# Loads of 128 rows, one load for keys, values and gates, stacked float32r scores from step 12, and a new order, in an mLSTM + MLP kernel

## The chip, the cores and the metric

The kernel runs on one core of a Trainium2 chip. The time is device microseconds of one launch of that core, and three timed runs and one profiled execution of the kernel before are at hand.

## The reference, cut to what matters

First a gated recurrent attention (mLSTM) over 768 tokens for 4 batches of 8 heads with 40 dimensions, then an MLP on its output with 320 inputs and 2048 hidden units.

```
for t in range(S):                       # C, n, m: state per batch and head
    m_new  = max(f[t] + m, i[t])
    C = exp(f[t] + m - m_new) * C + exp(i[t] - m_new) * v[t] k[t]^T
    n = exp(f[t] + m - m_new) * n + exp(i[t] - m_new) * k[t]
    y[t] = sigmoid(o[t]) * (C q[t]) / max(|n . q[t]|, 1)
h = x @ w_in                             # x: y with the heads side by side
out = (h * erf(softplus(h))) @ w_out
```

## The kernel before, in words

The recurrence is done in chunks of 128 tokens. A step `s` (0 to 23) is one chunk of one batch: `attention(s)`. Its scores, part `S` at L682, are eight products of 40 rows (keys against queries, one per head) in float32, each of which the chip runs as two instructions; the heads of a pair lie on rows 0 to 39 and 64 to 103. The scores are weighted on VectorE (L697), and `ph` multiplies them with the values (L719), adds the state's share (L715) and makes the state's update (L724). The result is gated (L759, L765), transposed on TensorE (`tr`, L777) and split into two float32r tiles `xh` and `xl` for the MLP.

The MLP takes two steps at a time (a block of 256 tokens) in two halves of the hidden units: 24 phases `f`. Each runs `up` (L990, eight float32r products of 256 columns for every 128 hidden units), a copy out of PSUM (`hb`, L999 on ScalarE or L1001 on VectorE), softplus and erf (L1009, L1013), their product with `h` (L1021), a split in two (`gh` L1027, `gl` L1032) and `dn` (L1067, L1068, L1070, of 320 columns). The first three phases (`FULL`) run `dn` in plain float32 instead (L1063). The weights arrive as 64-bit floats and are decoded piece by piece over the first 130 us: `val` on ScalarE (L810), `dec` and `hi`, `lo` on the engines that the sets `HI_DVE`, `LO_DVE` and `LO_PE` name; a `lo` in `LO_PE` is two products on TensorE (L833, L834).

A step's inputs come by three transfers, all issued on SP's queue: `load` (q and k, 104 rows of 4 KB, L566) and `loadv` (keys and values at L573, gates at L574). From step 4 on two more bring the decays (`dq`, L586), from step 8 on one more the cumulated gates (`bq`, L619). The store of the output is at L1094.

The order of the whole program is written by a planner, `Plan.issue`: each part has an engine, a cost and a due time (`target`, from `FIRST`, `PHASE` and `BEHIND`), `NUDGE` and `CLASS` shift due times of single parts, and a list simulation puts the parts in one fixed order per engine. Every engine, SP's queue among them, then works that order off without exchange. From step 9 on (`CLUSTER`) `tr` of step s-2, `S` of step s and `ph` of step s-1 are merged into one part `X` on TensorE. `CHAIN` fixes ScalarE's order of exponentials, softplus and erf.

The stacked form of the scores is in the code before, but for steps from `STACK = 24` on, so for none. It splits q and k into float32r parts, `hi` on ScalarE (`qkh`, L650) and `lo` on VectorE (`qkl`, L655), and ten transfers within SBUF (`stk`, L664 to L668) put hi, hi, lo of q over hi, lo, hi of k on 120 rows of one tile, so that one float32r product per head (L680) takes the place of L682.

Of the kernel before, what the change touches and what calls it, by code (L numbers as in the profile page):

```python
# [17 lines left out]
B, H, S, D = 4, 8, 768, 40  # L18
# [32 lines left out]
class Plan:  # L51
# [3 lines left out]
    RATE = 250.0  # L55
# [75 lines left out]
    def issue(self):  # L131
# [28 lines left out]
        for p in parts:  # L160
            p.late += NUDGE.get(p.name, CLASS.get(p.name.rstrip('0123456789'), 0.0) if int(p.name.lstrip('abcdefghijklmnopqrstuvwxyzSX_') or 0) >= CLUSTER else 0.0)
            for b in p.held:
                b.left += 1
# [105 lines left out]
FIRST = 43.4  # L269
PHASE = 17.5  # L270
BEHIND = 1.57
KEEP = {'raw': 2, 'qk': 2, 'kvo': 2}
HB_ACT = {0, 2, 3, 5}
HI_DVE = {'i00', 'i01', 'i31', 'o2', 'o4'}
BURST = {0, 2, 3, 6, 7, 8, 9, 10, 11, 12, 13, 14, 15, 16, 17, 18, 19, 20, 21, 22}
LO_DVE = {'i10', 'i21', 'o6', 'o9', 't2'}
LO_PE = {'i01', 'i20', 'o0', 't1', 't2', 't3'}
# [19 lines left out]
]  # L297
GL_POOL = {2, 4}
CLUSTER = 9
STACK = 24  # L300
CLASS = {}
PARTIAL = None
AFTER = 10
PREFER = 75.7
VG_POOL = {6, 7}
SK_ACT = {0, 1, 2}
Y_DVE = {0, 1, 5, 7}
NUDGE = {
# [57 lines left out]
def tile_mlstm_moe(  # L366
# [108 lines left out]
    def gate_chunk(c):  # L475
# [6 lines left out]
        @make(f'gload{c}', 'SP', 0.6, kb=128.0, new=[gtb], order=[step[4 * c - 6].S] if c > 1 else [])  # L482
        def load():
            v.gt = new(sb, [128, 2, L], F32, "gt")
            nc.sync.dma_start(v.gt, gates[:, :, c * L:(c + 1) * L])
# [716 lines left out]
```

## Time and profile before

| what | value |
|---|---|
| three runs | 481.88, 486.70, 486.58 us, median 486.58 |
| the profiled execution | 482.13 us, of which the span from first to last instruction is 480.4 us |
| mean granted TensorE clock | 0.985 of full speed |
| busy share of the span | TensorE 97%, weight loads 90%, VectorE 67%, ScalarE 69%, GpSimd 23% |
| moved by DMA | 51.01 MB, 106 GB/s over the span |

Busy times of TensorE are of pipelined instructions and overlap, so starts are compared, not durations. The profile's rows name an engine (PE is TensorE, PEld its weight loads, DVE VectorE, ACT ScalarE, POOL GpSimd, SP SyncE, which issues the transfers), a line of the kernel, an operation, and the tiles (output and inputs); x is a count. In brackets stands the idle time of the engine just before, and what ended it.

### The profile page before, as it was taken

What the parts mean: (1) busy time and instruction counts of PE and PEld (TensorE: products, weight loads), DVE (VectorE), ACT (ScalarE), POOL (GpSimd) and SP (SyncE); (2) the same over time, 40 slices, a digit from 0 to 9 for tenths busy, and PEclk for the clock granted to TensorE, in tenths of its full rate; (3) what the DMA queues carried; (4) which work ended last, traced back from release to release, by engine and by line L of the source; (5) the groups of instructions that cost most, each with busy time, mean ns of one, the idle gap of its engine ahead of it and who ended that gap; (6) DMA issues with size and microseconds to landing.
All of it is one profiled execution on the core that took longest, in us unless ns stands there. A gap on an engine that the chain in (4) does not pass through costs nothing.

```text
span 480.4 us, 13816 instructions
## 1 busy us (share of the span) xinstructions
PE 466.9 (97%) x6081; PEld 433.5 (90%) x6085; DVE 323.3 (67%) x548; ACT 331.4 (69%) x389; POOL 109.9 (23%) x103
## 2 busy tenths in 40 slices
PE   7998899999999999999999999999999999999997
PEld 3568769988899999999999999999999999999997
DVE  3488988725567869975877665966667665463562
ACT  4366976698769887858476487586488485475891
POOL 2113320310355410414220250320252121000000
PEclk9599989999999999999999999999999999999999
DMA  7999824322276155045324405145404000000000
GB/s 219 245 349 262 207 72 132 110 85 81 61 196 157 52 191 158 6 130 159 97 91 129 147 3 161 45 119 153 140 20 146 5 15 17 1 29 2 0 29 27
DMA packets 31660, 51.01 MB, mean 106 GB/s; under 512 B 3344, under 2 KB 21168, under 8 KB 31600
## 3 DMA queue, kind: packets, MB, share of 16 engines
q1 hardware_dynamic: 31600, 50.14, 36.2%
q8 instruction: 47, 0.77, 0.7%
q14 instruction: 13, 0.11, 0.1%
HBM read 46.05 MB, written 4.08 MB: 104 GB/s over the span
## 4 chain that ended last, share of the span: by engine, by line
PE 85%; DMA 8%; DVE 5%; issue 1%; ACT 0%; SPq 0%; ACTq 0%; DVEq 0%
PE h L990 35%; PE po L1067 10%; PE po L1070 10%; PE po L1068 10%; PE po L1063 6%; DMA raw<-in_w_in_dram 5%; PE pa L682 5%; PE pa L719 3%; PE pa L715 3%; DMA kvo<-in_kvo_dram 2%; PE pa L777 1%; PE pa L724 1%; DVE dm L697 1%; DMA qk<-in_qk_dram 1%; DVE hb L1021 1%
## 5 line engine op out<-in xcount | busy, mean ns | idle before, releaser
L990 PE MATMUL h<-xh,wh 128*128 128x256 f32 x576 | 159.2, 286 | 3.8 <-DVE hb L1001 2.4
L990 PE MATMUL h<-xl,wh 128*128 128x256 f32 x576 | 158.2, 284 | 1.4 <-issue 0.9
L990 PEld LDWEIGHTS h<-xh,wh 128*128 128x128 f32 x576 | 110.5, 192 | 5.2 <-DVE hb L1001 3.2
L990 PEld LDWEIGHTS h<-xl,wh 128*128 128x128 f32 x576 | 110.5, 192 | 2.1 <-issue 1.2
L990 PE MATMUL h<-xh,wl 128*128 128x256 f32 x384 | 108.9, 284 | 0.0
L1067 PE MATMUL po<-woh,gh 128*128 128x320 f32 x336 | 102.2, 316 | 0.0
L1068 PE MATMUL po<-wol,gh 128*128 128x320 f32 x336 | 99.8, 309 | 0.0
L1001 DVE COPY hb<-h 128x512 f32<-128x512 f32 x80 | 54.7, 688 | 56.4 <-PE h L990 55.8
L990 PEld LDWEIGHTS h<-xh,wl 128*128 128x128 f32 x384 | 73.8, 192 | 0.0
L1027 ACT ACTIVATE gh<-hb 128x1024 fp32r<-128x1024 f32 x42 | 44.3, 1056 | 36.3 <-DVE hb L1021 35.8
L1009 ACT ACTIVATE e<-hb 128x1024 f32<-128x1024 f32 x48 | 50.1, 1056 | 21.7 <-DVE hb L1001 21.3
L1067 PEld LDWEIGHTS po<-woh,gh 128*128 128x128 f32 x336 | 63.2, 188 | 1.1
L1068 PEld LDWEIGHTS po<-wol,gh 128*128 128x128 f32 x336 | 63.3, 188 | 0.0
L1021 DVE TENSOR_TENSOR hb<-e,hb 128x1024 f32<-128x1024 f32 x42 | 60.0, 1439 | 4.6 <-ACT e L1013 4.5
L1070 PE MATMUL po<-woh,gl 128*128 128x320 f32 x336 | 62.9, 309 | 0.0
L765 POOL TENSOR_TENSOR kvo<-kvo,den 128x320 f32<-128x320 f32 x20 | 19.2, 958 | 168.0 <-DVE kvo L759 168.0
L1070 PEld LDWEIGHTS po<-woh,gl 128*128 128x128 f32 x336 | 52.7, 188 | 0.0
L1032 DVE TENSOR_TENSOR gl<-hb,gh 128x1024 fp32r<-128x1024 f32 x40 | 49.7, 1252 | 3.2 <-ACT gh L1027 2.8
L1013 ACT ACTIVATE e<-e 128x1024 f32<-128x1024 f32 x48 | 49.2, 1054 | 0.3
L623 POOL TENSOR_TENSOR dm<-dm,aT 128x1024 f32<-128x1024 f32 x16 | 32.0, 2008 | 32.0 <-DVE aT L535 28.5
L1013 ACT ACT_TABLE_LOAD x29 | 37.2, 1283 | 0.5
L1009 ACT ACT_TABLE_LOAD x27 | 34.6, 1283 | 0.5
(110 smaller groups left out, 648.1 us busy)
## 6 DMA issues: line engine op xcount, KB each, us to landing
qk<-in_qk_dram SPq DMA_DIRECT2D x24, 416.0 KB
dm<-cum_dr SPq DMA_DIRECT2D x16, 512.0 KB
kvo<-in_kvo_dram SPq DMA_DIRECT2D x24, 324.0 KB
raw<-in_w_in_dram SPq DMA_DIRECT2D x8, 512.0 KB
kvo<-in_kvo_dram SPq DMA_DIRECT2D x24, 160.0 KB
out_dram<-o SPq DMA_DIRECT2D x24, 160.0 KB
raw<-in_w_out_dram SPq DMA_DIRECT2D x8, 320.0 KB
dq<-dec_dr SPq DMA_DIRECT2D x20, 128.0 KB
```

Of the source, the lines that this page charges most:

```text
L623: nc.gpsimd.tensor_tensor(v.dm, v.dm, G.aT[:, b].unsqueeze(2).to_broadcast([128, H, L]), op=ALU.add)
L990: nc.tensor.matmul(V.h[i][:, n % 2 * T:(n % 2 + 1) * T], w, m, start=(q == 0), stop=(q == len(ops) - 1))
L1001: nc.vector.tensor_copy(V.hb[:, i * 512:(i + 1) * 512], V.h[i])
L1009: nc.scalar.activation(V.e, V.hb, AF.Softplus)
L1013: nc.scalar.activation(V.e, V.e, AF.Erf)
L1021: nc.vector.tensor_tensor(V.g if full else V.hb, V.e, V.hb, op=ALU.mult)
L1027: nc.scalar.activation(V.gh, V.hb, AF.Copy)
L1032: (nc.gpsimd if f in GL_POOL else nc.vector).tensor_tensor(V.gl, V.hb, V.gh.bitcast(F32), op=ALU.subtract)
L1063: nc.tensor.matmul(K.po[b][:, c0:c0 + m], V.g[:, ts], w32[i][:, o:o + m], start=start and c0 == 0, stop=stop and at + m == w.stop)
L1067: nc.tensor.matmul(K.po[b], V.gh[:, ts], woh[:, w], start=start, stop=False)
L1068: nc.tensor.matmul(K.po[b], V.gh[:, ts], wol[:, w], start=False, stop=False)
L1070: nc.tensor.matmul(K.po[b], V.gl[:, ts], woh[:, w], start=False, stop=stop)
```

## The change

- `load` reads 128 rows in place of 104 for steps below `SPREAD = 9` (the rows past 103 are the next step's and are not used); `loadv` is one transfer in place of two, with the gates laid behind the values.
- `STACK` is 12, so steps 12 to 23 take the stacked form: per step 16 float32 instructions become 8 of float32r, and `qkh`, `qkl` and ten transfers are added.
- The planner gets other constants (its transfer rate, due times, nudges by class, loads not long before their due time), some parts are fixed in their order across steps, and all parts are ordered anew.
- Parts change engines: `HB_ACT`, `HI_DVE`, `LO_DVE`, `LO_PE`, `GL_POOL`, `VG_POOL`, `Y_DVE`.

```diff
-    RATE = 250.0
+    RATE = 370.0
...
+            if p.engine == 'SP' and p.new:
+                p.ready = max(p.ready, p.late - EAGER)
...
-FIRST = 43.4
+FIRST = 35.0
-BEHIND = 1.57
-KEEP = {'raw': 2, 'qk': 2, 'kvo': 2}
-HB_ACT = {0, 2, 3, 5}
-HI_DVE = {'i00', 'i01', 'i31', 'o2', 'o4'}
+BEHIND = 1.63
+KEEP = {'raw': 2, 'qk': 2, 'kvo': 3, 'part': 3, 'stk': 1}
+HB_ACT = {0, 6}
+HI_DVE = {'i00', 'i01', 'i31', 'o0', 'o2', 'o6', 'o9', 't1'}
-LO_DVE = {'i10', 'i21', 'o6', 'o9', 't2'}
-LO_PE = {'i01', 'i20', 'o0', 't1', 't2', 't3'}
+LO_DVE = {'i01', 'i10', 'i20', 'i21', 'i31', 'o1', 'o3', 'o4', 'o6', 'o7', 'o9', 't0'}
+LO_PE = {'i01', 'o1', 't1', 't2'}
...
-GL_POOL = {2, 4}
+GL_POOL = {3}
-STACK = 24
-CLASS = {}
+STACK = 12
+SPREAD = 9
+CLASS = {'sa': -6.7, 'sum': 3.2, 'X': -1.2, 'dn': -5.1, 'scan': 6.7, 'o': 4.9, 'ex': -0.5, 'qkl': 2.8, 'xl': -10.0, 'sp': 12.8, 'hb': 7.3, 'th': -15.7, 'w': 3.7, 'qkh': -1.5, 'qa': 4.4, 'er': -8.8, 'y': -6.4, 'xh': -16.9, 'gh': -3.5, 'load': 9.1, 'cumw': 8.0, 'add': 8.2, 'atc': -11.7, 'loadv': -13.4, 'gl': 2.5, 'yg': 0.6, 'mu': -0.6, 'vg': -4.4, 'gexp': -13.7, 'dq': 0.0, 'decw': 4.0, 'st': 2.4}
+EAGER = 200.0
-VG_POOL = {6, 7}
+VG_POOL = set()
-Y_DVE = {0, 1, 5, 7}
+Y_DVE = {0, 1, 5, 6, 8}
...
-            t = big("qk").rearrange("p (w n l) -> p w n l", w=2, n=NPR)
-            nc.sync.dma_start(t[0:QR], qk[c, b])
+            t = big("qk")
+            if s < SPREAD:
+                r = (c * B + b) * QR
+                nc.sync.dma_start(t, qk.rearrange("c b q w n l -> (c b q) (w n l)")[r:r + 128])
+            t = t.rearrange("p (w n l) -> p w n l", w=2, n=NPR)
+            if s >= SPREAD:
+                nc.sync.dma_start(t[0:QR], qk[c, b])
...
-            nc.sync.dma_start(n[:, DM:KVO], kvo[c, b][:, 0:KV])
-            nc.sync.dma_start(n[:, 0:DM], kvo[c, b][:, KV:KVO])
-            v.kn = n[:, DM:2 * DM].rearrange("p (h d) -> p h d", d=D)
-            v.v1 = n[:, 2 * DM:KVO].rearrange("p (h d) -> p h d", d=V1)
-            v.th = n[:, 0:DM]
-            v.y = n[:, 0:DM + 64]
+            nc.sync.dma_start(n[:, 0:KVO], kvo[c, b])
+            v.kn = n[:, 0:DM].rearrange("p (h d) -> p h d", d=D)
+            v.v1 = n[:, DM:KV].rearrange("p (h d) -> p h d", d=V1)
+            v.th, v.y = n[:, KV:KVO], n[:, 0:DM + 64]
...
+    for s in range(CLUSTER - 1, steps):
+        for x, y in zip(step[s - 1].grabs, step[s].grabs):
+            y.order.append(x)
+    taken = [phases[i].taken[j] for kind, i, j in CHAIN if kind == 'sp' and i < phases_]
+    for x, y in zip(taken, taken[1:]):
+        y[0].order.append(x[0])
+        y[1].order.append(x[2])
+        y[2].order.append(y[1])
```

`grabs` are a step's `load`, `loadv`, `dq` and `vg`; `taken` are a pair of `up` parts and the copy of the first. `CHAIN` and `NUDGE` are replaced by longer lists of the same kind; the cost of `loadv` and the sizes (`kb`) of a few transfers change in the planner alone.

## Rows read from the trace of the kernel before

**Rows 1.** The page: shares of the chain of waits that ended last, by engine.

```profile
PE 85%; DMA 8%; DVE 5%; issue 1%; ACT 0%; SPq 0%; ACTq 0%; DVEq 0%
```

**Rows 2.** Busy time of each engine by stretch: start and end of the stretch, its length, busy us of PE, PEld, DVE, ACT and POOL (with counts), the granted clock, the DMA engines' share, GB/s.

```profile
0.00:36.00 36.00, 30.93 (x448) 17.77 (x451) 20.82 (x54) 17.41 (x33) 7.62 (x16) 0.86 0.94 271
36.00:60.00 24.00, 20.15 (x246) 18.20 (x245) 21.20 (x45) 18.92 (x30) 8.21 (x9) 0.99 0.94 234
60.00:72.00 12.00, 12.00 (x186) 8.07 (x184) 10.40 (x18) 8.78 (x14) 3.27 (x3) 0.88 0.26 73
180.00:402.00 222.00, 221.00 (x3096) 216.22 (x3096) 160.78 (x254) 150.46 (x162) 57.32 (x48) 1.00 0.32 94
```

**Rows 3.** TensorE's weight loads in time order, around one merged part X: start, duration of the group, line. The rows of L1067 and L1068 stand behind it.

```profile
295.25 0.40 PEld L777 LDWEIGHTS pa<-ident,kvo 128*128 128x128 f32 x3
295.82 0.97 PEld L682 LDWEIGHTS pa<-qk 40*128 40x128 f32 x16 [0.17 <-issue]
296.91 0.16 PEld L715 LDWEIGHTS pa<-state,qk 104*32 104x32 f32 x8
298.52 0.19 PEld L1067 LDWEIGHTS po<-woh,gh 128*128 128x128 f32 x1
298.63 0.19 PEld L1068 LDWEIGHTS po<-wol,gh 128*128 128x128 f32 x1
```

**Rows 4.** The same view where float32r loads follow transposes, where they start after idle time, and where L715 follows a float32r product.

```profile
44.07 0.31 PEld L777 LDWEIGHTS pa<-ident,kvo 128*128 128x128 f32 x3
44.35 0.19 PEld L990 LDWEIGHTS h<-xh,wh 128*128 128x128 f32 x1
...
58.09 0.19 PEld L990 LDWEIGHTS h<-xh,wh 128*128 128x128 f32 x1 [1.37 <-DVE hb L1001]
58.20 0.19 PEld L990 LDWEIGHTS h<-xl,wh 128*128 128x128 f32 x1
...
76.73 0.19 PEld L990 LDWEIGHTS h<-xl,wh 128*128 128x128 f32 x1
77.06 0.16 PEld L715 LDWEIGHTS pa<-state,qk 104*32 104x32 f32 x8
```

**Rows 5.** Products in time order: two of 256 columns (L990) and two of 320 (L1067, L1068), each pair one pitch apart.

```profile
292.44 0.28 PE L990 MATMUL h<-xh,wh 128*128 128x256 f32 x1
292.56 0.28 PE L990 MATMUL h<-xl,wh 128*128 128x256 f32 x1
...
293.78 0.31 PE L1068 MATMUL po<-wol,gh 128*128 128x320 f32 x1
293.93 0.31 PE L1067 MATMUL po<-woh,gh 128*128 128x320 f32 x1
```

**Rows 6.** The chain of waits in order of time: one float32 `dn` (ten instructions, two for each of five products that make up 1280 columns), and the two products of `lo` of `i20` on TensorE.

```profile
64.06 2.47 PE po L1063 x10
...
60.89 1.71 PE pa L833 x2
62.60 0.37 PE pa L834
```

**Rows 7.** Products of the first MLP phases that begin after idle time, and an ACT row that waits for a weight piece.

```profile
36.62 0.39 PE L990 MATMUL h<-xh,wh 128*128 128x256 f32 x1 [0.27 <-ACT xh L790]
47.95 0.38 PE L990 MATMUL h<-xh,wh 128*128 128x256 f32 x1 [1.10 <-ACT xh L790]
53.30 0.39 PE L990 MATMUL h<-xh,wh 128*128 128x256 f32 x1 [0.78 <-DVE hb L1001]
58.10 0.39 PE L990 MATMUL h<-xh,wh 128*128 128x256 f32 x1 [1.20 <-DVE hb L1001]
...
17.35 0.66 ACT L878 ACTIVATE bits<-raw 128x512 f32<-128x512 f32 x1 [4.91 <-DMA raw<-in_w_in_dram]
```

**Rows 8.** Groups of instructions by line: busy us, mean ns of one, idle before.

```profile
L1027 ACT ACTIVATE gh<-hb 128x1024 fp32r<-128x1024 f32 x42 | 44.3, 1056 | 36.3 <-DVE hb L1021 35.8
L1032 DVE TENSOR_TENSOR gl<-hb,gh 128x1024 fp32r<-128x1024 f32 x40 | 49.7, 1252 | 3.2 <-ACT gh L1027 2.8
L843 DVE TENSOR_TENSOR wol<-bits,woh 128x512 fp32r<-128x512 f32 x2 | 1.5, 759 | 0.3 <-ACT woh L824 0.3
L950 DVE CAST woh<-w 128x512 fp32r<-128x512 f32 x2 | 0.8, 422 | 0.0
L690 DVE TENSOR_TENSOR vg<-kvo,dm 128x328 f32<-128x328 f32 x18 | 11.1, 624 | 3.5 <-ACT dm L611 1.8 <-POOL dm L632 1.2 <-DMA kvo<-in_kvo_dram 0.2
L1001 DVE COPY hb<-h 128x512 f32<-128x512 f32 x80 | 54.7, 688 | 56.4 <-PE h L990 55.8
```

**Rows 9.** SP: one load of q and k (issued at 156.54) and the stretch of 2.60 us in which it moves alone (columns as in rows 2); an issue of `loadv`; what SP's queue waited for (us in total, times, longest us).

```profile
157.50:160.10 2.60, 2.60 (x135) 2.54 (x136) 2.46 (x4) 2.57 (x4) 0.12 (x1) 1.00 0.55 169
...
310.87 0.43 SPq L573 DMA_DIRECT2D kvo<-in_kvo_dram  x1
...
SPq L1094 <- ACT o L1087: 137.1, 14, 31.2
SPq L586 <- DVE state L734: 49.7, 11, 9.5
```

**Rows 10.** Products in time order where a row of `up` stops in the middle.

```profile
154.24 0.39 PE L990 MATMUL h<-xh,wh 128*128 128x256 f32 x1 [0.42 <-DVE hb L1001]
...
216.84 0.39 PE L990 MATMUL h<-xl,wh 128*128 128x256 f32 x1 [0.95 <-issue]
```

More of the change, by code (lines that the diff above doesn't have):

```diff
@@ L268 @@
 FILL = (0.0, 45.0, 0.2)
-FIRST = 43.4
+FIRST = 35.0
 PHASE = 17.5
-BEHIND = 1.57
-KEEP = {'raw': 2, 'qk': 2, 'kvo': 2}
-HB_ACT = {0, 2, 3, 5}
-HI_DVE = {'i00', 'i01', 'i31', 'o2', 'o4'}
-BURST = {0, 2, 3, 6, 7, 8, 9, 10, 11, 12, 13, 14, 15, 16, 17, 18, 19, 20, 21, 22}
-LO_DVE = {'i10', 'i21', 'o6', 'o9', 't2'}
-LO_PE = {'i01', 'i20', 'o0', 't1', 't2', 't3'}
+BEHIND = 1.63
+KEEP = {'raw': 2, 'qk': 2, 'kvo': 3, 'part': 3, 'stk': 1}
+HB_ACT = {0, 6}
+HI_DVE = {'i00', 'i01', 'i31', 'o0', 'o2', 'o6', 'o9', 't1'}
+BURST = {0, 1, 2, 4, 5, 7, 8, 9, 10, 11, 12, 13, 14, 15, 16, 17, 18, 19, 20}
+LO_DVE = {'i01', 'i10', 'i20', 'i21', 'i31', 'o1', 'o3', 'o4', 'o6', 'o7', 'o9', 't0'}
+LO_PE = {'i01', 'o1', 't1', 't2'}
 CHAIN = [
@@ L294 @@
     ('sp', 19, 0), ('sp', 19, 1), ('er', 19, 0), ('er', 19, 1), ('sp', 20, 0), ('sp', 20, 1), ('er', 20, 0),
[2 rows of a table removed]
[2 rows of a table added]
 ]
-GL_POOL = {2, 4}
+GL_POOL = {3}
 CLUSTER = 9
-STACK = 24
-CLASS = {}
+STACK = 12
+SPREAD = 9
+CLASS = {'sa': -6.7, 'sum': 3.2, 'X': -1.2, 'dn': -5.1, 'scan': 6.7, 'o': 4.9, 'ex': -0.5, 'qkl': 2.8, 'xl': -10.0, 'sp': 12.8, 'hb': 7.3, 'th': -15.7, 'w': 3.7, 'qkh': -1.5, 'qa': 4.4, 'er': -8.8, 'y': -6.4, 'xh': -16.9, 'gh': -3.5, 'load': 9.1, 'cumw': 8.0, 'add': 8.2, 'atc': -11.7, 'loadv': -13.4, 'gl': 2.5, 'yg': 0.6, 'mu': -0.6, 'vg': -4.4, 'gexp': -13.7, 'dq': 0.0, 'decw': 4.0, 'st': 2.4}
+EAGER = 200.0
 PARTIAL = None
-AFTER = 10
-PREFER = 75.7
-VG_POOL = {6, 7}
+AFTER = 9
+PREFER = 83.4
+VG_POOL = set()
 SK_ACT = {0, 1, 2}
-Y_DVE = {0, 1, 5, 7}
+Y_DVE = {0, 1, 5, 6, 8}
 NUDGE = {
[51 rows of a table removed]
[52 rows of a table added]
 }
@@ L467, in p_mask @@
         nc.scalar.activation(early.eye, ident, AF.Copy)
-    steps, halves = PARTIAL or (B * NC, 2 * NK)
+    steps, phases_ = PARTIAL or (B * NC, 2 * NK)
     step = [SimpleNamespace() for _ in range(B * NC)]
@@ L480, in gate_chunk @@
         A, C, Y = range(3)
-        @make(f'gload{c}', 'SP', 0.6, kb=128.0, new=[gtb], order=[step[4 * c - 6].S] if c > 1 else [])
+        @make(f'gload{c}', 'SP', 0.6, kb=170.0, new=[gtb], order=[step[4 * c - 6].S] if c > 1 else [])
         def load():
@@ L561, in attention @@
         v.pe = []
-        @make(f'load{s}', 'SP', 0.45, kb=416.0, new=[qkb])
+        @make(f'load{s}', 'SP', 0.45, kb=512.0, new=[qkb])
         def load():
-            t = big("qk").rearrange("p (w n l) -> p w n l", w=2, n=NPR)
-            nc.sync.dma_start(t[0:QR], qk[c, b])
+            t = big("qk")
[5 more added lines that the diff above has]
+                nc.sync.dma_start(t[0:QR], qk[c, b])
             v.qk, v.q, v.k = t, t[:, 0], t[:, 1]
         v.load = load
-        @make(f'loadv{s}', 'SP', 0.8, kb=484.0, new=[kvb])
+        v.grabs = [load]
+        @make(f'loadv{s}', 'SP', 0.45, kb=484.0, new=[kvb])
         def loadv():
             n = big("kvo")
-            nc.sync.dma_start(n[:, DM:KVO], kvo[c, b][:, 0:KV])
-            nc.sync.dma_start(n[:, 0:DM], kvo[c, b][:, KV:KVO])
-            v.kn = n[:, DM:2 * DM].rearrange("p (h d) -> p h d", d=D)
-            v.v1 = n[:, 2 * DM:KVO].rearrange("p (h d) -> p h d", d=V1)
-            v.th = n[:, 0:DM]
-            v.y = n[:, 0:DM + 64]
+            nc.sync.dma_start(n[:, 0:KVO], kvo[c, b])
+            v.kn = n[:, 0:DM].rearrange("p (h d) -> p h d", d=D)
+            v.v1 = n[:, DM:KV].rearrange("p (h d) -> p h d", d=V1)
+            v.th, v.y = n[:, KV:KVO], n[:, 0:DM + 64]
+        v.grabs.append(loadv)
         if c > 0:
@@ L587, in dqp @@
                                       dec_dr[c, b:b + 1].rearrange("o (p j) l -> o j p l", j=2)[:, j].to_broadcast([n, NPR, L]))
+            v.grabs.append(dqp)
         ex, sel = [], []
@@ L692, in attention @@
             vg.append(vgp)
+            v.grabs.append(vgp)
         for j in range(2):
@@ L867, in weights_tail @@
         at = [slice(0, 64), slice(64, 128)]
-        @make(f'tail{pair_}', 'SP', 1.0, kb=512.0, new=[b])
+        @make(f'tail{pair_}', 'SP', 1.0, kb=800.0, new=[b])
         def load():
@@ L1002, in mlp @@
                 copies.append(copy)
+                if i == 0:
+                    v.taken = getattr(v, 'taken', []) + [[copy, up]]
+                else:
+                    v.taken[-1].append(up)
                 v.up.append(up)
@@ L1106, in tile_mlstm_moe @@
         weights_out(u)
-    for f in range(halves):
+    for f in range(phases_):
         mlp(f)
@@ L1115, in tile_mlstm_moe @@
     for kind, i, j in CHAIN:
-        if i >= (halves if kind in ('sp', 'er') else steps if kind == 'ex' else -(-steps // B)):
+        if i >= (phases_ if kind in ('sp', 'er') else steps if kind == 'ex' else -(-steps // B)):
             continue
```

119 rows, old and new, of tables (CHAIN, NUDGE) are left out of this document.

## The prediction

> **What bounds the kernel now.** I read the chain of waits first: 85% of it is TensorE and 8% are transfers [rows 1]. Then the busy times by stretch [rows 2]: from 180 to 402 us TensorE is busy for 221.0 of 222 us at full clock, so work taken off it there comes off the end, and new work on another engine costs nothing until TensorE waits for it. The first 60 us are another regime: the DMA engines have a share of 0.94, VectorE is busy for 21.2 of 24 us between 36 and 60, and TensorE runs fill-in work and waits. The first product of the MLP starts at 36.62 us [rows 7].
>
> The sum is made against the profiled execution, 482.13 us. The median of the three runs is 486.58, which is 4.45 more; the lowest is 481.88. I forecast at the level of the profiled one.
>
> **Stacked scores.** All twelve steps lie in the saturated stretch. Today a step's scores run from the first load at 295.82 to the first load of `ph` at 296.91, 1.09 us, with 0.17 us idle ahead [rows 3]. The new form is eight float32r loads and products. Its price is bounded by two things that the trace shows. Products of 256 columns follow each other by 0.12 us, those of 320 by 0.15 [rows 5]: 64 columns cost 27 ns, and a line through both puts 128 columns at 0.066 us. But each product also loads 128 columns of weights, and where such loads aren't held up by a product, they still stand 0.11 us apart (58.09 to 58.20, and 298.52 to 298.63) [rows 3, 4]. I take 0.11, since the load is the nearer row: same type, same 128 columns. `ph` follows the last float32r load by 0.33 us (76.73 to 77.06) [rows 4], so a step costs 7 x 0.11 + 0.33 = 1.10 us, no less than now. What goes is the idle time ahead: float32r loads follow transposes at 0.11 or less (three transposes from 44.07, then 44.35) [rows 4]. Saving: 0.17 us a step, 12 x 0.17 = 2.0 us. The good end, 0.066, gives 7 x 0.066 + 0.33 = 0.79 and saves 0.47 a step, 5.6 us. The bad end is that 128 columns of float32r go at the float32 rate on a full array: 1280 columns took 2.47 us [rows 6], so 1024 take 1.98, a loss of 0.89 - 0.17 = 0.72 a step, 8.6 us. Every float32r row here has 256 columns or more, so the trace doesn't exclude it, but all of those are a single instruction each, and so are the new ones.
>
> [...]
>
> **What the scores need.** `qkh` on ScalarE, 12 x 1.06 = 12.7 us, and `qkl` on VectorE, 12 x 1.25 = 15.0 us [rows 8]. From 180 to 402 us these engines have 71.5 and 61.2 us free [rows 2], which covers both; if the cover is gone, `gh` and `gl` are late and `dn` waits for them. The ten transfers per step hold SP for about 10 x 0.43 = 4.3 us [rows 9] and move 960 KB, 11.5 MB in all; by the share of 0.32 at 94 GB/s [rows 2] this adds about 0.18 to the DMA share there. All of it is hidden if it is issued in time. I take 0; the range keeps a loss (the slower rival).
>
> **Loads.** q and k of a step, 416 KB, moved in 2.60 us at a share of 0.55 [rows 9], so it leaves engines free, and 24 rows more might ride along. But in the first 60 us the share is 0.94 already, and the nine longer loads add 0.86 MB, 3.2 us at 271 GB/s [rows 2]. I take 0, between a gain of 2 us (if the longer form spreads better) and a loss of 3. One issue of `loadv` less is 0.43 us of SP per step [rows 9], on no chain that ended last.
>
> [...]
>
> **Parts that change engines.** [...] VectorE gets six more `lo` (0.76), three `hi` (0.42), two `vg` (0.62) and, net, eight copies `hb` (0.69): 4.6 + 1.3 + 1.2 + 5.5 = 12.6 us [rows 8], nearly all before 150 us. Between 36 and 60 it has 2.8 us free [rows 2].
>
> **The new order.** It can return idle time only. Between 36 and 60 us TensorE idles for 24 - 20.15 = 3.85 us [rows 2], four stops of which make 0.27 + 1.10 + 0.78 + 1.20 = 3.35 [rows 7]. Ahead of 36 us it idles for 5.1 and also runs fill-in work, and ScalarE stands 4.91 us for a weight piece [rows 7]. An earlier start of the MLP is thus worth anything from 0 to some 8 us; against it stand the bytes, which don't get fewer, and VectorE. I take -2.0 (about half of the four stops) with -8 and +5 (the 3.85 again, and a stop of a microsecond) as ends. Later on there are stops of 0.42 and 0.95 us [rows 10]; -0.5.
>
> **Sum:** -2.0 + 0 + 0 - 1.0 - 2.0 - 0.5 = -5.5, so 482.13 - 5.5 = 476.6 us.
>
> **The rivals.**
> - *The start moves by much and the scores are cheaper:* products at 0.066 us, -5.6, and a start that is 5 us earlier, with -1.5 for the rest: 470.0 us. For it: the fill-in work and the idle time ahead of 36 us. Against it: a DMA share of 0.94, and loads 0.11 us apart. [...] Chance 0.23, to 465.
> - *VectorE binds the start:* 12.6 us more on an engine with 2.8 us free eats the 2.0 and the 1.0, and `up` waits for `hb` more than today's 0.78 and 1.20 [rows 7]: 482.1 - 2.5 + 2 = 482 us. For it: the two stops that end with `hb`. Against it: the moves need not fall between 36 and 60 us. Chance 0.18.
> - *Slower, the stacked tiles come late:* `X` holds `tr`, `S` and `ph`, TensorE's order is fixed, so a tile that is late stops everything. Its way is long (load, ScalarE, VectorE, ten transfers on SP), and SP's queue is in order: today it stands up to 31.2 us for an output and 9.5 us for the state [rows 9], and what is behind waits along. At 1.5 us a step it would be 18 - 5.5: 494.6 us. It decides from 0.46 us a step on (5.5 / 12). Against it: other loads have lived behind such waits without a stop of TensorE in this stretch. Chance 0.12.
> - *The scores don't get cheaper at all:* float32r of 128 columns at the float32 rate, +8.6 in place of -2.0: 487.2 us. Chance 0.05.
>
> **How the numbers follow.** The forecast, 472 to 480.5, has 0.42. The range of 8 in 10 reaches from 465 to 487: it takes in the faster rival, the VectorE one and the low end of the late tiles. About 1% (5 us) is what a measurement of this kernel can tell from no change; the runs before differ by as much. Faster by over 1%: the faster rival, and most of the forecast (against the profiled 482.13 it needs less than 477.3, against the median less than 481.7): 0.60. Same: the rest of it, the VectorE rival, a little of the others: 0.25. Slower: late tiles and dear scores, 0.15.
>
> **What would show it.** In the changed kernel the loads of the stacked product stand 0.11 us apart with no idle time ahead (0.07 or 0.08: the first rival; 0.2 or more: the last). TensorE's waits name no transfer into a stacked tile; if they do, the slower rival is at work. The two products of `i20` are gone from about 60 us. The first product of the MLP starts before 36.6 us, and the idle time between 36 and 60 us is below 3.85; if `hb` ends more of it than now, VectorE binds. VectorE and ScalarE end some 15 to 28 and 8 to 13 us busier. The prediction is wrong if the end moves by more than the starts of MLP phases and the twelve steps together account for.

## The result, and the profile after

The change makes the kernel slower by a little: 486.8 us in the median against 482.36 of the kernel before, ratio 1.0093 [1.0072, 1.0114]. The forecast was 476.6 us and faster; the time lies inside its range of 465 to 487, and the direction is wrong. Ratios here leave out runs more than 1.5% above the fastest of the same kernel. The profiled execution of after has a span of 484.2 us against 480.4.

The page of after, first the shares of the chain of waits by engine (to hold against [rows 1]), then the DMA queues (kind: packets, MB, share of 16 engines).

```profile
PE 76%; DMA 9%; DVE 5%; ACT 4%; issue 2%; SPq 2%; POOL 1%; ACTq 0%; DVEq 0%; POOLq 0%
...
q1 hardware_dynamic: 34387, 62.82, 42.0%
q8 instruction: 47, 0.77, 0.7%
```

Busy time by stretch in after, columns as in [rows 2].

```profile
0.00:36.00 36.00, 29.32 (x444) 16.69 (x447) 25.09 (x61) 18.25 (x36) 8.41 (x16) 0.91 0.94 321
36.00:60.00 24.00, 21.75 (x243) 19.65 (x245) 22.70 (x50) 18.45 (x28) 3.78 (x5) 0.93 0.61 206
180.00:402.00 222.00, 215.22 (x2961) 212.32 (x2959) 169.38 (x265) 158.26 (x173) 53.77 (x47) 0.99 0.50 147
```

Read it from the top. "Issue" has grown to 2% of the chain: time in which an engine waited for nothing that the profile names. The start is about as long: between 36 and 60 us TensorE idles for 24 - 21.75 = 2.25 us where it was 3.85 [rows 2], but ahead of 36 us for 36 - 29.32 = 6.68 us where it was 5.07; the first product of the MLP comes at 35.90 us. The loss is in the stretch that was full: 215.22 us busy of 222, where it was 221.00 [rows 2]. The transfers' share there rose from 0.32 to 0.50, the 0.18 that the prediction worked out.

I summed, for every product, the time to the start of the next. From before to after TensorE's idle time grows by 6.6 us and all its work together shrinks by some 3, which leaves the 3.8 us of the two spans. The starts of the MLP phases tell where: until the twelfth one after has lost nothing (244.3 us against 244.7), at the next it is 6.2 us behind. In between lies one place. TensorE's products in time order there, in after (the last row is a second, short stop of the same kind, further on):

```profile
252.10 1.09 PE L692 MATMUL pa<-stk 120*128 120x128 f32 x8
253.12 0.35 PE L728 MATMUL pa<-state,qk 104*32 104x82 f32 x8
...
254.33 0.47 PE L737 MATMUL pa<-vg,kvo 128*32 128x41 f32 x31
260.02 0.24 PE L737 MATMUL pa<-vg,kvo 128*8 128x41 f32 x1 [5.22 <-issue]
260.19 0.64 PE L1084 MATMUL po<-woh,gh 128*128 128x320 f32 x1
260.62 0.47 PE L1085 MATMUL po<-wol,gh 128*128 128x320 f32 x1
...
353.27 0.25 PE L737 MATMUL pa<-vg,kvo 128*32 128x41 f32 x5 [0.74 <-issue]
```

and the stretches of 2 us around it (columns as above; the last three are granted clock, DMA share, GB/s):

```profile
252.00:254.00 2.00, 2.00 (x81) 1.93 (x83) 1.97 (x3) 1.12 (x3) 0.00 (x0) 1.00 0.97 182
254.00:256.00 2.00, 0.80 (x75) 0.67 (x66) 1.04 (x2) 0.00 (x0) 0.00 (x0) 1.00 0.90 295
256.00:258.00 2.00, 0.00 (x0) 0.00 (x0) 0.00 (x0) 0.00 (x0) 0.00 (x0) 1.00 1.05 243
258.00:260.00 2.00, 0.00 (x0) 0.00 (x0) 0.00 (x0) 1.62 (x3) 0.00 (x0) 0.96 1.10 281
260.00:262.00 2.00, 1.98 (x8) 1.90 (x9) 1.64 (x6) 0.17 (x1) 0.61 (x1) 0.50 0.90 296
262.00:264.00 2.00, 2.00 (x11) 2.00 (x11) 1.91 (x4) 0.00 (x0) 0.35 (x2) 0.69 0.83 234
```

TensorE stops for 5.22 us one product short of the end of a run of 32 like products, all of the same operands: no data can be missing. After it the granted clock is 0.50, and products of 320 columns follow each other by 0.27 us in place of 0.15 [rows 5]. The DMA engines' share is 0.90 to 1.10 while it stands. On queue q8, "instruction", 47 packets carry 0.77 MB, 16.4 KB each; TensorE ran 5976 products and 5982 loads, 254 for each such packet; in e8 below, with 5662 of each, it is 44 packets, 257 for each. So that queue brings TensorE its program, a block of some 256 instructions at a time, and the page counts its packets as it counts those of the data on q1, as a share of the 16 DMA engines (0.7% and 42.0%). By the trace's packets, the block that holds the missing product began to move at 257.24 and was there at 258.51; TensorE went on 1.5 us later still. Every other block of this trace began to move while TensorE was still 60 to 295 instructions short of it; at 257.24 TensorE had come to its first instruction and stood.

The second thing that the transfers do shows on ScalarE. What ScalarE waited for between 180 and 402 us in after (us in total, times, longest us); in the kernel before, its only wait for a transfer there is 1.7 us, once. Part of it is the order: e4 below, in after's order but without the stacked transfers, has 16.6 us in four waits for the loads of `kvo`.

```profile
ACT kvo L651 <- DMA kvo<-in_kvo_dram: 29.2, 7, 6.7
ACT L1026 <- DMA stk<-part: 4.2, 1, 4.2
```

### The profile page after: what moved, and what is told of

It reads as the page before. It is cut to its first block, busy times and chain, and to the rows that moved or that the text cites. A ratio compares the mean times of both kernels' runs of the same rounds, so it can differ in the third digit from the quotient of the medians.

```text
span 484.2 us, 13900 instructions
## 1 busy us (share of the span) xinstructions
PE 464.1 (96%) x5976; PEld 433.8 (90%) x5982; DVE 347.7 (72%) x581; ACT 337.8 (70%) x391; POOL 100.5 (21%) x94
## 4 chain that ended last, share of the span: by engine, by line
PE 76%; DMA 9%; DVE 5%; ACT 4%; issue 2%; SPq 2%; POOL 1%; ACTq 0%; DVEq 0%; POOLq 0%
PE h L1003 32%; PE po L1084 10%; PE po L1085 10%; PE po L1087 10%; DMA raw<-in_w_in_dram 4%; PE po L1080 3%; PE pa L728 2%; PE pa L692 2%; PE pa L732 2%; DMA kvo<-in_kvo_dram 2%; DMA qk<-in_qk_dram 2%; PE pa L694 1%; DMA raw<-in_w_out_dram 1%; PE pa L790 1%; PE pa L737 1%
## 5 line engine op out<-in xcount | busy, mean ns | idle before, releaser
L1014 DVE COPY hb<-h 128x512 f32<-128x512 f32 x88 | 60.2, 687 | 49.3 <-PE h L1003 45.5
L1038 DVE TENSOR_TENSOR hb<-e,hb 128x1024 f32<-128x1024 f32 x42 | 54.4, 1305 | 12.3 <-ACT e L1030 12.1
L635 POOL TENSOR_TENSOR dm<-dm,aT 128x1024 f32<-128x1024 f32 x16 | 35.3, 2209 | 45.8 <-DMA dm<-cum_dr 24.7
L644 POOL TENSOR_SCALAR_AFFINE_SELECT dm<-dm 128x1024 f32<-128x1024 f32 x16 | 20.5, 1282 | 89.4 <-ACT dm L639 85.2
L778 POOL TENSOR_TENSOR kvo<-kvo,den 128x320 f32<-128x320 f32 x19 | 15.2, 798 | 111.1 <-DVE kvo L772 56.5
```

The costliest lines, as they stand in the source:

```text
L635: nc.gpsimd.tensor_tensor(v.dm, v.dm, G.aT[:, b].unsqueeze(2).to_broadcast([128, H, L]), op=ALU.add)
L644: nc.gpsimd.affine_select(out=v.dm, in_=v.dm, pattern=[[0, H], [1, L]], compare_op=ALU.is_ge, fill=0.0, base=0, channel_multiplier=-1)
L1014: nc.vector.tensor_copy(V.hb[:, i * 512:(i + 1) * 512], V.h[i])
L1038: nc.vector.tensor_tensor(V.g if full else V.hb, V.e, V.hb, op=ALU.mult)
```

## The experiments

Two theories stood at first. **Late block:** the stacked form's transfers, with the loads issued among them, fill the DMA engines, and a block of TensorE's program comes late. **Order:** the newly searched order, or the loads, lose the time, and the stacked form has little to do with it. Ratios are to the kernel before.

### Shifting the program: e1_shift126, e2_shift48

The first 21 (or 8) fill-in products are split into four each, so that all later instructions stand 126 (or 48) places on in TensorE's program. The data, the transfers and the order are as in after.

```
-        nc.tensor.matmul(early.bank, warm, ...[128, 512])
+        for i in range(4 if early.fills <= 21 else 1):       # e2: 8
+            nc.tensor.matmul(early.bank[:, i * m:(i + 1) * m], warm, ...[128, m])
```

> The changed kernel with its first 21 fill-in products (512 columns each, in the first 10 us) written as four of 128 columns: same TensorE time, same order, same transfers, but every later instruction stands 126 places further in TensorE's program. Theory (TensorE ran out of program: its next block of instructions came late while the DMA engines were full): the stop of 5.2 us at 254.8 us goes or moves and shrinks, and the time falls by 5 to 8 us, to 479 to 482. Rival (the stop is a wait for data, or a late stacked tile): it stays at the same product, 484 to 488. Rival (VectorE binds the start): no change, 484 to 488.

> The same with 8 fill-in products split, a shift of 48 places. Theory: the block's end falls 48 instructions earlier, inside the same merged part, and its request some 3 us earlier; the stop shrinks to 2 to 3 us or goes, 480 to 484. Rivals: 484 to 488 with the stop where it was.

Measured: 1.007 [1.003, 1.011] and 1.0135 [1.0071, 1.0199]. The times that the theory named did not come, the medians are 484.7 and 489.4 us. But in both the stop at 254.8 us is gone, and others stand elsewhere. Products in time order, first of e1, then of e2:

```profile
140.99 0.28 PE L1006 MATMUL h<-xh,wh 128*128 128x256 f32 x1 [1.07 <-issue]
...
234.61 0.41 PE L1087 MATMUL po<-woh,gh 128*128 128x320 f32 x1 [1.85 <-issue]
```

```profile
142.63 0.93 PE L697 MATMUL pa<-qk 40*128 40x128 f32 x10
146.37 0.60 PE L697 MATMUL pa<-qk 40*128 40x128 f32 x6 [2.81 <-issue]
```

Each cuts a run of like products, of another kind each time. What they share is the place in the program. For the next table TensorE's instructions are counted in every trace (loads, products and those of its queue; a product that the trace misses counts with its load), and the place is the remainder modulo 256. It has all stops of TensorE over 0.3 us, after 60 us, that have no releaser, in all fourteen traces; the one of the kernel before is the short one of [rows 10].

| kernel | stop, us | ends at | place | packet of q8 landed | ends later by |
|---|---|---|---|---|---|
| before | 0.95 | 216.84 | 193 | 215.51 | 1.33 |
| after | 5.22 | 260.02 | 193 | 258.51 | 1.51 |
| after | 0.74 | 353.27 | 195 | 351.88 | 1.39 |
| e1 | 1.07 | 140.99 | 192 | 139.61 | 1.38 |
| e1 | 0.37 | 146.36 | 194 | 145.05 | 1.31 |
| e1 | 1.85 | 234.61 | 193 | 232.98 | 1.63 |
| e2 | 2.81 | 146.37 | 194 | 144.88 | 1.49 |
| e5 | 3.15 | 266.35 | 193 | 264.89 | 1.46 |
| e5 | 0.61 | 359.61 | 195 | 358.25 | 1.36 |
| e6 | 1.23 | 146.00 | 193 | 144.54 | 1.46 |
| e6 | 1.27 | 217.30 | 193 | 216.07 | 1.23 |
| e10 | 0.98 | 215.83 | 193 | 214.49 | 1.34 |

All stand at one place, within 3 of 256, and each ends 1.2 to 1.6 us after a packet of q8 has landed. (e1's stop of 1.34 us before 196.21, which the profile puts down to ScalarE, stands there too, 1.50 us behind a landing.) In no trace does TensorE run the instruction of that place less than 1.1 us after the landing. So the place in the program decides, not the work, and the packet is what TensorE waits for. This is the late block. e1's first MLP product comes at 38.42 us, 2.5 later than in after; whether the split fill-in products cost this is not shown, since e12, with after's start, has it at 37.39.

### Taking the transfers away: e3_light, e7_late, and adding them: e6_traffic

e3 issues one of the five transfers per stacked tile and takes the scores from 40 rows; it leaves out the low parts of q and k. e7 keeps the form, but uses it from step 18 on only, and shrinks split and transfers of steps 12 to 17 to one element. e6 is the kernel before with ten idle transfers of the stacked form's size per step from 12 on.

```
 e3 -                    nc.sync.dma_start(t[D:2 * D, 0], hi[js, 0])      # and three more
    +                    (left out; products over t[0:D])
 e7 -                    if stacked:
    +                    if s >= LATE:                                    # LATE = 18
 e6 +                    nc.sync.dma_start(scratch[s - 12, j, 0, :, 0:1024], wh.bitcast(F32)[0:D, 0, 0:1024])   # and four of half the size
```

> The changed kernel with one of the five transfers into each stacked tile left in (the float32r hi parts of q and k, 40 rows), the scores from these 40 rows: 8 of 10 transfers per step are gone and the output lacks the low parts of the scores; TensorE's program keeps its length. Theory with the transfers of the stacked tiles as what held up the block of instructions: the stop at 254.8 us shrinks below 2 us, 479 to 483. If the full engines at that time come from the other loads (two steps' loads stand together there): the stop stays at 4 to 6 us, 484 to 487. Rival (stacked tiles late): gains too, but with the waits of TensorE on stacked tiles gone.

> The changed kernel in its own order with the stacked scores from step 18 on and the scores as before in steps 12 to 17 (their split and transfers shrunk to one element): the stacked tiles' traffic starts about where the stop was. Price of the scores: 6 x 0.17 = 1.0 us below the version without stacked scores (482.8), so 481 to 482.5 if no block of instructions comes late, 483 to 486 if the traffic of the six steps is enough to hold one up.

> The kernel before, in its order and with its scores, with ten more transfers for each of steps 12 to 23, of the rows and sizes of the stacked tiles (960 KB a step) from a weight tile to a scratch in HBM that nobody reads, issued behind the step's load of q and k. No engine waits for them. Theory (full DMA engines hold up TensorE's program): new stops of TensorE after 150 us that no data releases, 3 to 8 us in all, 485 to 490. Rival (only the way from q and k to the stacked tile, or the other order, costs): no such stops, 481 to 484.

Measured: e3 0.9983 [0.9955, 1.001], e7 0.9988 [0.9956, 1.002], e6 1.0034 [0.9996, 1.0072]. In e3 and e7 no stop without a releaser is left. The stretch from 180 to 402 us of e3, e7 and e6, in this order:

```profile
180.00:402.00 222.00, 220.37 (x3081) 215.84 (x3080) 178.54 (x273) 161.40 (x175) 55.53 (x48) 1.00 0.39 113
```

```profile
180.00:402.00 222.00, 220.71 (x3139) 217.03 (x3139) 172.28 (x273) 156.81 (x176) 55.35 (x49) 1.00 0.42 124
```

```profile
180.00:402.00 222.00, 220.25 (x3083) 215.44 (x3082) 160.25 (x254) 149.90 (x160) 57.36 (x48) 1.00 0.47 142
```

So the transfers are what costs, at a share of 0.50 with bursts of 0.9 to 1.1. But e6 has 0.47 and loses 0.3%, with an interval from 0 to 0.7%, less than the 485 to 490 us that were expected (its two stops without a releaser are in the table, 1.23 and 1.27 us): the bytes alone don't do it. All twelve stops of the table stand at one place, within 3 of 256: a burst has to meet it, and in e6, whose transfers leave for HBM, nothing waits for the bytes.

### The part X cut below a block: e8_whole, e12_whole_one

A merged part X runs through 278 instructions in 3.0 us, which is over one block. Taking the state's update in 40 columns at once leaves out 32 of them; e8 does it in every step, e12 in step 14 alone, which is the one that stopped.

```
-                for d in (slice(0, 32), slice(32, D)):
+                for d in (slice(0, D),):                     # e12: if s == 14
```

> The changed kernel with the update of the state in 40 columns at once instead of 32 and 8: 32 instructions fewer in every merged part of steps 1 to 19, which falls from 278 to 246, below one block of 256. Theory: a merged part now meets one block's end at most and the requests lie further ahead in time; the stops shrink to 0 to 3 us, 479 to 483, if the wider products cost no time of their own. Rival (the stop is a wait for data): 484 to 488.

> The kernel after, with the state's update of step 14 alone taken in 40 columns at once (16 products fewer than 32; it is the update in the merged part in which TensorE stopped for 5.22 us). Theory 'a block of TensorE's program came late': nothing that moves by DMA changes, the block's end falls 16 instructions later in the program's text from there on, so the part still spans a block's end and a stop of some size remains there (1 to 6 us), while later ones move; 480 to 487 us. Rival 'the part X as such, by the data it waits for, stops': the stop stays at 5.2 us within 0.3 and at the same product. If the stop is gone and none takes its place, this version is at 480 to 481, the best of those measured.

(In e12 the text's 16 are products; with their loads it is 32 instructions.) Measured: 1.0017 [0.9967, 1.0068] and 1.006 [1.0031, 1.0089]. e8 has no stop without a releaser in its trace, and pays some 0.13 us per merged part for dearer updates; the trace is of a run of 482.4 us, and the twelve times reach from 479.6 to 490.1, so other runs may have some. e12 removes the one stop: from the twelfth phase start (244.3 us in after, 247.2 in e12) to the next (268.9 and 265.3) it takes 18.1 us in place of 24.5. So the data of this part was there, against the rival. At the block's place, now 32 instructions on in the work, only 0.2 us are lost (two products 0.34 us apart at 260.19 in place of 0.15), and still the time is not the 480 to 481 of the last sentence: the ratio is better than after's by 0.3% alone, with intervals that overlap. (This execution of e12 was 1.5 to 2.8 us behind after's up to the stop; at 276.5 us both are level.) Its products later on, and ScalarE's rows ahead of the first of them:

```profile
276.48 0.39 PE L1003 MATMUL h<-xh,wh 128*128 128x256 f32 x1 [3.40 <-DVE hb L1014]
313.83 0.39 PE L1003 MATMUL h<-xh,wh 128*128 128x256 f32 x1 [1.55 <-DVE hb L1014]
```

```profile
268.41 0.47 ACT L651 ACTIVATE kvo<-kvo 128x320 f32<-128x320 f32 x1 [6.28 <-DMA kvo<-in_kvo_dram]
268.90 1.28 ACT L1026 ACT_TABLE_LOAD   x1
270.19 2.00 ACT L1026 ACTIVATE e<-hb 128x1024 f32<-128x1024 f32 x2
272.21 1.28 ACT L1030 ACT_TABLE_LOAD   x1
273.51 2.00 ACT L1030 ACTIVATE e<-e 128x1024 f32<-128x1024 f32 x2
```

So the stop had covered a second lateness. ScalarE stands 6.28 us for a load of gates that SP issued at 257.86 and that landed 10.5 us later; softplus and erf of the MLP stand behind it in ScalarE's fixed order, VectorE's `hb` behind them, and `up` behind that. In after the same wait is 6.67 us (ScalarE's table above), but TensorE had lost its 5.2 us by then and didn't notice. How long ScalarE stands is not the measure. In e4, without the stacked transfers, it stands as long for the same load:

```profile
258.69 0.47 ACT L651 ACTIVATE kvo<-kvo 128x320 f32<-128x320 f32 x1 [6.28 <-DMA kvo<-in_kvo_dram]
```

but there the load took 6.1 us from its issue at 252.63, and no product waits; in e8, with all the transfers, it took some 7.7 us, and none waits either. What the transfers add is the later issue and the slower landing, and e12 is one trace in which this reached TensorE. The 1.55 us at 313.83 are not theirs: e4 has the same stop, 1.55 us before 307.05.

### The other parts alone: e4_unstack, e5_rows104, e10_rows128

e4 is after's order with the scores as before, split and transfers shrunk to one element. e5 is after with the old loads of 104 rows. e10 is the kernel before with the loads of 128 rows in steps 0 to 8 and nothing else.

```
 e4  -                    if stacked:
     +                    if False:
 e5  -SPREAD = 9
     +SPREAD = 0
 e10 -            nc.sync.dma_start(t[0:QR], qk[c, b])
     +            if s < 9:                                            # r: the step's first row
     +                nc.sync.dma_start(t, qk.rearrange(...)[r:r + 128])
```

> The changed kernel in its own order, with the scores of steps 12 to 23 as before (16 float32 instructions from the q and k tile), the split and the transfers shrunk to one element. My price of the scores: 12 x 0.17 = 2.0 us more on TensorE; the stop at 254.8 us moves, since the program is 16 instructions longer per step and the transfers are gone: 481 to 484. If the stacked form itself costs (late tiles, full engines): below 480. If it pays much (0.47 us a step): 486 or more.

> The changed kernel in its own order with q and k of steps 0 to 8 loaded as 104 rows again; TensorE's program is the same, place for place. My price of the longer loads is 0 (gain of 2 to loss of 3 us): the time stays within 1.5 us of the changed kernel's 486.8, and the stop at 254.8 us is there. If the longer loads paid: 488 to 489. If they cost: 484.

> The kernel before with loads of 128 rows for q and k in steps 0 to 8 alone. Theory 'the 128-row form itself moves faster': in the order of after the 104-row form lost 8 us before 95 us, so here the start should come earlier, with the first MLP product before 36.6 us and -2 to -5 us at the end, and 0:36 at more than 271 GB/s. Rival 'the order of after was fitted to these loads, the form by itself is worth nothing': 0 within 1.5 us, same GB/s.

Measured: e4 0.9995 [0.9966, 1.0024], e5 1.0254 [1.0184, 1.0325], e10 0.9991 [0.9962, 1.0019]. All of the change without the stacked form is worth nothing that can be measured. From e4 to after, in the same order, the spans grow by 4.6 us (479.6 to 484.2), and the traces name 3.9 of them: 5.2 and 0.7 for the two late blocks, 1.6 for the lower clock behind the first, 0.8 for a wait for `hb` at 200.42, less 2.9 for the scores and 1.55 for the stop at 307.05, which after doesn't have. In that part of the change the loads and the order hang together. The first two stretches of e5, then of e10:

```profile
0.00:36.00 36.00, 29.92 (x442) 16.80 (x443) 24.09 (x58) 17.32 (x33) 7.53 (x15) 0.86 0.93 275
36.00:60.00 24.00, 17.57 (x204) 14.50 (x203) 17.60 (x43) 17.22 (x27) 3.33 (x5) 0.86 0.86 225
```

```profile
0.00:36.00 36.00, 29.24 (x434) 16.84 (x435) 20.17 (x52) 17.27 (x32) 7.36 (x16) 0.87 0.94 312
36.00:60.00 24.00, 20.67 (x252) 18.29 (x253) 21.02 (x47) 18.22 (x29) 7.56 (x9) 0.99 0.61 200
```

The longer form does move faster: 312 GB/s against 271 [rows 2] in e10 (the unused rows counted), and the share between 36 and 60 us falls from 0.94 to 0.61. But in the old order nothing comes earlier by it: the first MLP product is at 37.56 us, where it is at 37.62 in e6, which has the start of before. In after's order the loads matter, and without them phase 2 starts at 94.2 us in place of 86.0. e5's median, 493.9 us, is 7 us above after's, where 1.5 at most was expected; it has the late blocks of after at the same products, of 3.15 and 0.61 us (table above). That e10 gains nothing is the rival's outcome; that its bytes move faster is the theory's.

### The stacked form alone: e9_stackonly, e11_both

The kernel before with `STACK = 12`, and that with e10's loads as well; the planner places the new parts by its old constants.

```
-STACK = 24
+STACK = 12
```

> The kernel before with STACK = 12 alone: stacked scores in steps 12 to 23, everything else (constants of the planner, engines of the parts, loads) as before; the planner places the new parts itself. Theory 'the scores pay 2 us, and their transfers cost a late block of TensorE's program only where the block's end falls into a full stretch': TensorE's stacked scores save about 1.9 us, the order isn't fitted to the new parts, so stops come in anywhere; I expect 0 to +4 us against before, and any stop of TensorE over 1 us in the last two thirds has no data releaser. Rival 'it was the new order, not the scores': -2 us, with no such stop.

> The kernel before with both: loads of 128 rows in steps 0 to 8 and STACK = 12, the planner's constants as before. If the two are independent, the time is the sum of what they do alone (against before) within 2 us; if the start moves the later bursts against the block ends of TensorE's program, it departs from the sum by the stops without a data releaser, read in its trace.

Measured: 1.0329 [1.028, 1.0378] and 1.023 [1.0155, 1.0305]. Both theories miss: e9 loses some 15 us, and none of it to late blocks. What TensorE waited for in e9 from 180 to 402 us, and a piece of its chain of waits in time order (start, us, what):

```profile
PE h L990 <- DVE hb L1001: 8.9, 5, 2.9
PE h L990 <- ACT xh L790: 2.4, 2, 1.5
PE po L1070 <- DVE gl L1032: 2.0, 2, 1.2
```

```profile
195.43 5.09 DMA qk<-in_qk_dram
...
200.59 1.07 ACT part L650
...
201.69 1.23 DVE part L655
202.92 0.61 DVE hb L1001
...
203.57 1.46 PE h L990 x10
```

This is the preparation of a stacked tile on the path that sets the end: the load of q and k issued behind ten transfers takes 5.09 us, ScalarE and VectorE stand in their orders for it, and the MLP's copy `hb` stands behind them. The new order takes most of this away: with it the stacked form costs 1.0% (after against e4), without it 3.3%. That e11 loses less than e9 and e10 together (2.3% against 3.2) is not explained here; the six times of e11 reach from 490.0 to 499.9 us, and the difference lies within that.

## Why the prediction was wrong

- **Stacked scores, right in size, the reason only in part.** The loads of the stacked product stand 0.111 us apart, no idle time ahead, as "0.11" said. The scores take 0.84 us in the chain of waits before `ph`, where the old ones took 1.09; from the last product before `tr` to the first of `ph` a step is shorter by 0.24 us, 2.9 us for twelve, where the sum had 2.0.

The chain of waits of after, one step, and of before, the same step (start, us, what):

```profile
207.88 0.33 PE pa L790 x3
208.21 0.84 PE pa L692 x8
209.05 0.28 PE pa L728 x8
```

```profile
209.84 0.33 PE pa L777 x3
210.17 1.09 PE pa L682 x16
211.26 0.28 PE pa L715 x8
```

The sum had the idle time ahead go because the loads are float32r. e3's are float32r too, but of 40 rows as in before, and there it stays. The weight loads of the scores in after, then in e3:

```profile
252.08 0.97 PEld L692 LDWEIGHTS pa<-stk 120*128 120x128 f32 x8
```

```profile
253.38 0.96 PEld L688 LDWEIGHTS pa<-stk 40*128 40x128 f32 x8 [0.17 <-issue]
```

So it goes with the 120 rows. Why, no run shows. (It also makes a step of e3 0.19 us dearer than one of after, so e3 came back to the level of before in spite of it.)

- **What the scores need, wrong: this is the step that failed.** "All of it is hidden if it is issued in time. I take 0." The 0.18 of DMA share was right as a mean, and the mean was the mistake. The transfers come in bursts, with the step's loads, in which the share is 0.9 to 1.1, and what moves beside them waits: a block of TensorE's program (5.22 us, and about 1.6 more at the lower clock, 2 us at 0.50 and 2 at 0.69), and the loads for which ScalarE stands in its order (29.2 us, where it is 1.7 in before and 16.6 in e4; in e12 such a wait cost TensorE 3.40 us). Taking eight of ten transfers away (e3), or half of the steps (e7), brings the kernel back to the level of before. The issues were also dearer for SP than taken: 0.71 us each where 0.43 was assumed, so ten hold it for over 7 us.
- **The slower rival** had the place right (X stops, behind a long way over SP), but not the mechanism: no wait of TensorE in after names a stacked tile, as "what would show it" asked. In e9, in the old order, the rival's long way does decide, by way of `hb`.
- **Loads, 0: right in sum for the old order (e10), wrong in after's.** There they carry about 8 us of the start (e5). In e10 the engines' share between 36 and 60 us falls by 0.33, from 0.94 [rows 2] to 0.61, 7.9 us of 24, so the longer form does leave the engines freer; why, no run shows.
- **Parts that change engines and the new order: the gain of 3.5 us is not there.** In this trace the idle time between 36 and 60 us fell by 1.6 us, and the first MLP product came 0.7 us earlier, which looks like the -2.0. But the idle time ahead of 36 us rose by the same 1.6, and the start differs as much between executions. e3, e4, e7 and e12 have after's start, and in them the idle time between 36 and 60 us is 3.9, 3.5, 1.9 and 2.5 us and the first product comes at 36.0 to 37.4. Where it is low the granted clock is low too (0.93 in after and e12, 0.86 in e7, 1.00 in e3 and e4), which fits products that are slower and fill the time. e4's row:

```profile
36.00:60.00 24.00, 20.51 (x243) 18.20 (x245) 22.78 (x49) 18.70 (x28) 3.88 (x6) 1.00 0.61 202
```

VectorE, busy for 22.70 of 24 us there, did not bind: `hb` ends 0.4 us of TensorE's waits in after and 1.6 in e4, where it was 2.0 (over the span VectorE is 24 us busier, ScalarE 6). e4 shows that neither this nor the 1.0 of `lo` reaches the end: without the stacked form the time is that of before. No run shows the 1.0 that the sum has for `lo` of `i20`: from its two products to the scores behind them it is 2.21 us in before, where the granted clock is 0.50 from 60 to 62 us, and 1.18 in e10, where it is 1.00 from 60 to 72 us; in after and e4 they are gone from there, and e4's ratio is 0.9995.
- **The test that was named** ("wrong if the end moves by more than the starts of MLP phases and the twelve steps together account for") came out as wrong at one place, the 6.2 us between two phase starts.

That the stop is a late block of the program rests on e1 and e2 (it moves with the program alone), the table of twelve stops (one place, and a packet of q8 that landed just before each end), e3 and e7 (it goes with the transfers), e8 and e12 (it goes with 32 instructions). That ScalarE's wait comes next is read from one trace, that of e12. No version run here beats the kernel before: the best ones, e3 (which leaves work out), e7 and e10, can't be told from it.

## What to carry to other kernels

When work is moved from a full engine to transfers, don't judge the cover by the mean DMA share: lay the new transfers beside the loads that are issued with them, and ask what else moves in that burst, the engine's own program included. Here the share was 0.50 in the mean and 0.90 to 1.10 at the stop. TensorE ran a merged part of 278 instructions in 3.0 us, over one block of its program, so a stop marked "issue" in the middle of a run of like products is to be held against the DMA share just before it. And a stop that is removed may have covered the next one: after e12's 5.2 us were gone, 3.40 us of another wait stood in their place.

## What was not expected of the hardware

- TensorE stopped for 5.22 us with all its data there. Twelve such stops, of 0.37 to 5.22 us, stand in seven kernels at instructions whose place in the program has the same remainder modulo 256, within 192 to 195. The blocks move on queue q8 (47 packets, 0.77 MB); TensorE goes on 1.2 to 1.6 us after the landing, and in fourteen traces no packet begins to move more than 299 instructions ahead of that place.
- After the stop of 5.22 us in after the granted clock was 0.50 for 2 us and 0.69 in the next two.
- Loads of 40 rows behind transposes of 128 start 0.17 us after the engine was free, in float32 (before) and in float32r (e3) alike; those of 120 rows start with no idle time ahead (after).
- A load of 484 KB, keys, values and gates, took 10.5 us from issue to landing among the stacked transfers in e12, and 6.1 us in e4 without them; q and k, 416 KB, were issued at 156.54 and landed, moving alone, at 160.10 [rows 9].
